# Four landing tiles, a summed turn of w_out, batch 0's Q scaled on ScalarE, and the quarters of the second stage in a row

## The chip, the cores and the metric

One core of a Trainium2 chip runs the whole program, one launch, all data in fp32. The metric is the device time of one execution in microseconds; three runs of the kernel before gave 676.89, 678.52 and 679.67 us (median 678.52). The profiled execution took 679.15 us.

Engines are named as in the profile: PE is TensorE (PEld its weight loads), DVE is VectorE, ACT is ScalarE, POOL is GpSimd, SP is SyncE, which here issues nearly all DMAs.

## What is computed

Three stages follow each other. Attention: 4 batches, 8 heads, 576 positions of 64 elements, with a causal mask over blocks of 64. Its output, as 2304 tokens of 512, goes through a dense layer with a maximum over three products, and that output through a mixture of experts with top-1 routing and a skip.

```python
scores = q @ k.T / sqrt(64), masked where block_i < block_j
x = softmax(scores) @ v                                # 2304 x 512
h = maximum(maximum(x @ w1, x @ w2), x @ w3)           # 2304 x 768
x2 = h @ w_out                                         # 2304 x 512
do = x2 @ w_skip > 0;  e = argmax(x2 @ w_gate);  gate = max softmax(x2 @ w_gate)
out = x2 + do * gate * (relu(x2 @ m2_w1[e]) @ m2_w2[e])  # 8 experts, 1024 wide
```

## The kernel before, in words

Tokens are handled in 9 chunks of 256. The scores of one head and up to 128 queries are a *half-unit*; the loop at L588 runs over the 192 half-units. For each one, `s_scores` multiplies Q by K (L295 for batch 0, L299 and L301 for the others), takes the negated maximum of each row (L306), applies the exponential with that maximum as bias (L314); `s_norm` scales the rows, `s_trans` turns them (L347), `s_pv` multiplies by V (L364). The half-units are two heads deep, and the four stages of neighbouring half-units overlap.

Precision: the dense layer splits each fp32 operand into a high and a low fp32r part. Batch 0's Q and K are used as plain fp32 (L295): K is loaded by L228 and Q by L229, the 64 rows and the 9 mask rows apart, so four DMAs for each of 12 (chunk, head pair) groups, eight of them with 256 queries and four with 64. For batch 0 the factor 0.125 is not on Q: it stands in the exponential's `scale` and on the maxima (L311 where a score has one part, folded into the minimum of L309 where it has two). For the other batches `prep` puts it on Q (L269).

The weights of the dense layer come as the raw 64-bit words of the host's arrays, 512 KB a piece: 18 pieces for w1 to w3 and 6 for w_out. `wprep` loads a piece into one of three landing tiles `raw` (L157, L164) and decodes it: ACT takes the absolute value (L146), DVE does four passes (L147 to L150), ACT copies the high part (L167), DVE subtracts the low one (L168). A landing tile is free again after L150. `routes` turns w_out (each 128 x 128 block by two matmuls, high and low part against a fp32r identity, L183), splits it and multiplies it by the router's weights, for the logits of later chunks.

Which work stands where: the attention phase is written in program order, with priorities, and a scheduler with its own model of durations places the instructions of each engine; each engine then runs its list in that order, and waits at the head of its list. The dense layer's steps (`moe_steps`, matmuls of L379 and L417) are handed out between half-units by a credit. SP's list of DMAs is also in order: a DMA waits there for its buffer to be free.

The second stage (`Moe2`) is in a fixed order. Seven tiles of 128 tokens each take four *quarters* of expert weights of 1 MB: s = 0 and 1 are the halves of the first layer, s = 2 and 3 those of the second; `self.seq` (L756) lists the 28 quarters, and loads, splits (ACT L838, DVE L843) and matmuls (L864, 12 a quarter) follow it. Between them `turn_h` turns the relu of a half (L852, copies L855 and L856) and `turn_x` turns a gathered tile of tokens. In the first tiles the order is (0,0) (0,1) (0,2) (1,0) (0,3) (1,1) and on; the relu of each half (L944, L946) stands on ACT behind the split of a quarter that comes five later.

## Time and profile before

| what | value |
|---|---|
| median of three runs | 678.52 us |
| profiled execution, its own time | 679.15 us |
| its span, first to last instruction | 677.4 us |
| busy in the span: PE, DVE, ACT, POOL | 654.1, 474.3, 384.7, 162.7 us |
| mean granted TensorE clock | 0.990 |

The profiled execution's time is 1.75 us longer than its span, and 0.63 us over the median. A busy PE is not PE at its peak: a matmul's record is longer than its step to the next one, so short waits are hidden in the busy time.

### The profile page before, as it was taken

What the parts mean: (1) busy time and instruction counts of PE and PEld (TensorE: products, weight loads), DVE (VectorE), ACT (ScalarE), POOL (GpSimd) and SP (SyncE); (2) the same over time, 40 slices, a digit from 0 to 9 for tenths busy, and PEclk for the clock granted to TensorE, in tenths of its full rate; (3) what the DMA queues carried; (4) which work ended last, traced back from release to release, by engine and by line L of the source; (5) the groups of instructions that cost most, each with busy time, mean ns of one, the idle gap of its engine ahead of it and who ended that gap; (6) DMA issues with size and microseconds to landing.
All of it is one profiled execution on the core that took longest, in us unless ns stands there. A gap on an engine that the chain in (4) does not pass through costs nothing. (4 is left out here: it accounts for less than half of the span.)

```text
span 677.4 us, 13700 instructions
## 1 busy us (share of the span) xinstructions
PE 654.1 (97%) x4820; PEld 553.7 (82%) x4820; DVE 474.3 (70%) x1405; ACT 384.7 (57%) x1012; POOL 162.7 (24%) x293
## 2 busy tenths in 40 slices
PE   6789999899999999999999999999999999999996
PEld 4548875689888998998997898889799889788885
DVE  4788998865677865776666656766675277599991
ACT  5677887757355554645444456454444163387861
POOL 2112122344113113221120224222021067221101
PEclk9979999999999999999999999999999999999999
DMA  7754444531222124223111132320210299399920
GB/s 201 183 167 137 149 149 145 180 78 56 79 74 57 52 68 149 78 60 110 28 28 60 60 91 82 122 82 21 83 37 6 78 337 328 107 323 379 380 96 12
DMA packets 78353, 83.18 MB, mean 123 GB/s; under 512 B 9150, under 2 KB 57694, under 8 KB 78282
## 3 DMA queue, kind: packets, MB, share of 16 engines
q1 hardware_dynamic: 76538, 79.19, 36.6%
q0 software_dynamic: 1744, 3.09, 1.3%
q8 instruction: 39, 0.64, 0.4%
q14 instruction: 32, 0.26, 0.1%
HBM read 71.58 MB, written 11.44 MB: 123 GB/s over the span
## 5 line engine op out<-in xcount | busy, mean ns | idle before, releaser
L379 PE MATMUL ps_h<-x,w 128*128 128x256 f32 x1944 | 277.1, 291 | 1.0 <-DVE hm L386 0.6
L379 PEld LDWEIGHTS ps_h<-x,w 128*128 128x128 f32 x1944 | 249.6, 192 | 11.1 <-issue 4.0
L314 ACT ACTIVATE p<-sc,nm 64x288 f32<-64x288 f32 (+9 forms) x192 | 95.4, 499 | 35.5 <-DVE nm L306 7.8
L306 DVE TENSOR_REDUCE nm<-sc 64x1 f32<-64x288 f32 (+9 forms) x192 | 85.2, 450 | 32.1 <-PE sc L301 20.4
L347 PE MATMUL tp<-cst_sb,p 128*128 128x128 f32 (+1 forms) x480 | 89.1, 280 | 5.7 <-ACT pT L349 3.4
L347 PEld LDWEIGHTS tp<-cst_sb,p 128*128 128x128 f32 (+1 forms) x480 | 57.0, 143 | 28.1 <-issue 12.5
L364 PE MATMUL pv<-pT,vt 128*64 128x128 f32 (+1 forms) x960 | 73.7, 277 | 0.7 <-ACT pT L349 0.7
L349 ACT COPY pT<-tp 128x256 f32<-128x256 f32 (+4 forms) x112 | 44.8, 400 | 42.9 <-PE tp L347 38.2
L843 DVE TENSOR_TENSOR lo<-raw,hi 128x1024 fp32r<-128x1024 f32 (+1 forms) x50 | 67.8, 1401 | 0.0
L391 POOL TENSOR_TENSOR h_l<-hm,h_h 128x256 fp32r<-128x256 f32 x52 | 45.8, 880 | 86.5 <-ACT h_h L390 86.1
L364 PEld LDWEIGHTS pv<-pT,vt 128*64 128x64 f32 x960 | 50.8, 139 | 17.4 <-issue 5.2
L274 POOL TENSOR_TENSOR kl<-kq,kh 64x512 fp32r<-64x512 f32 (+3 forms) x36 | 36.8, 1022 | 93.2 <-ACT kh L273 93.1
L838 ACT CAST hi<-raw 128x2048 fp32r<-128x2048 f32 x28 | 53.5, 1911 | 5.4 <-DMA raw<-in_m_w_dram 5.4
L351 DVE COPY pT<-tp 128x256 f32<-128x256 f32 (+4 forms) x80 | 35.4, 445 | 26.9 <-PE tp L347 24.3
L335 DVE TENSOR_SCALAR p<-p,r 128x320 f32<-128x320 f32 (+9 forms) x104 | 48.6, 468 | 4.5
L295 PE MATMUL sc<-kn,kq 73*64 73x288 f32 (+4 forms) x96 | 41.4, 532 | 8.3 <-DMA kq<-in_kq_dram 5.5
L299 PE MATMUL sc<-kh,q 128*128 128x288 f32 (+9 forms) x144 | 48.4, 341 | 0.0
L367 DVE TENSOR_TENSOR x<-pv,x 128x128 fp32r<-128x128 f32 (+1 forms) x80 | 21.7, 271 | 36.2 <-ACT x L366 35.7
L318 POOL MEMSET p<- 128x64 f32 (+1 forms) x96 | 14.4, 154 | 128.9 <-PE tp L347 107.2
L301 PE MATMUL sc<-kl,q 128*128 128x288 f32 (+9 forms) x144 | 44.1, 309 | 0.0
L417 PE MATMUL ps_y<-wo_h,h_h 128*128 128x512 f32 x108 | 43.9, 407 | 0.1
L417 PE MATMUL ps_y<-wo_h,h_l 128*128 128x512 f32 x108 | 42.8, 396 | 0.0
(206 smaller groups left out, 1045.2 us busy)
## 6 DMA issues: line engine op xcount, KB each, us to landing
raw<-in_m_w_dram SPq DMA_DIRECT2D x28, 1024.0 KB
raw<-in_w_dram SPq DMA_DIRECT2D x18, 512.0 KB
kq<-in_kqT_dram SPq DMA_DIRECT2D x16, 512.0 KB
vt<-in_v_dram SPq DMA_DIRECT2D x16, 320.0 KB
x<-y SPq DMA_DIRECT2D x18, 256.0 KB
out_dram<-y SPq DMA_DIRECT2D x18, 256.0 KB
raw<-in_w_out_dram SPq DMA_DIRECT2D x6, 512.0 KB
kq<-in_kqT_dram SPq DMA_DIRECT2D x8, 384.0 KB
```

Source lines behind the costliest of these rows:

```text
L299: nc.tensor.matmul(ps[:nq, 0:hi - lo], gd["q1"][:, j, q0:q0 + nq], gd["kh"][:, j, lo:hi], start=True, stop=False)
L306: nc.vector.tensor_reduce(nm[:nq, n:n + 1], pss[n][:nq, 0:hi - lo], axis=AX.X, op=ALU.max, negate=True)
L314: nc.scalar.activation(pt[:nq, lo:hi], pss[n][:nq, 0:hi - lo], AF.Exp, bias=nm[:nq, 0:1], scale=scale, accum_out=su[:nq, n:n + 1])
L335: nc.vector.tensor_scalar(pt, pt, r[:nq, 0:1], None, op0=ALU.mult)
L347: nc.tensor.transpose(tp[:, t, 0:nq], h["p"][:nq, (t0 + t) * P:(t0 + t + 1) * P], ident[:nq, :nq])
L349: nc.scalar.copy(pT[:, t0:t0 + n, 0:nq], tp[:, 0:n, 0:nq])
L364: nc.tensor.matmul(pv[64 * jj:64 * jj + 64, 0:nq], vt[:, t, 64 * jj:64 * jj + 64], hd[k - 1 + jj]["pT"][:, t, 0:nq], start=(t == 0), stop= ...
L379: nc.tensor.matmul(ps, a[:, d, :], x[:, d, :], start=(n == 0), stop=(n == 3 * ND - 1))
L391: (nc.vector if c == NCH - 1 and f >= NF - 2 else nc.gpsimd).tensor_tensor(h_l[:, f, :], prev, h_h[:, f, :], op=ALU.subtract)
L417: nc.tensor.matmul(ps, a[:, f, hs], x[:, f, :], start=(n == 0), stop=(n == 3 * NF - 1))
L838: self.nc.scalar.copy(self.w(q)[0], self.raw_of(q))
L843: eng.tensor_tensor(lo[:, :, a:b], raw[:, :, a:b], hi[:, :, a:b], op=ALU.subtract)
```

## The change

Five edits. (1) The decode has four landing tiles in place of three. (2) `routes` first adds the two parts of w_out on DVE (a tile `w`, 128 x 512 fp32) and turns the sum with one fp32 transpose a block; the fp32r identity and its copy on POOL are gone. (3) For batch 0, `prep` multiplies Q by 0.125 in place on ACT, once a group, with a high priority; `prep(0)` is called before the first loop step. The factor is gone from the exponential and the maxima: L311's instruction is gone, and L309 becomes a plain minimum. (4) The table of constants is loaded in three DMAs, the identity early, the triangle and the small tables later. (5) The quarters of the first tile stand in a row, (0,0) (0,1) (0,2) (0,3) (1,0) (1,1) (1,2) (2,0) (1,3) and on; the turns of the first tile's second half and of the second tile's tokens move with them.

```diff
--- before.py
+++ after.py
@@ -73,12 +73,11 @@
     table = dram.tile([NE * CAP, 2], F32, name="table")
     tdram = dram.tile([28, 2], I32, name="tdram")
 
-    cst_sb = const.tile([P, 2 * P + 8 + 10 + 8], F32, name="cst_sb")
+    cst_sb = const.tile([P, P + 8 + 10 + 8], F32, name="cst_sb")
     ident = cst_sb[:, 0:P]
-    rev8 = cst_sb[:, 2 * P:2 * P + 8]
-    fold = cst_sb[0:20, 2 * P + 8:2 * P + 18]
-    base8 = cst_sb[:, 2 * P + 18:2 * P + 26]
-    ident_r = const.tile([P, P], F32R, name="ident_r")
+    rev8 = cst_sb[:, P:P + 8]
+    fold = cst_sb[0:20, P + 8:P + 18]
+    base8 = cst_sb[:, P + 18:P + 26]
     tri = const.tile([P, P], BF16, name="tri")
     ones = const.tile([P, P], BF16, name="ones")
     tid = const.tile([P, NT // P], F32, name="tid")
@@ -95,7 +94,7 @@
 def _moe1_phase(tc, nc, const, small, g):
     kqT, kq0, v = g["kqT"], g["kq0"], g["v"]
     ident, rev8, fold, base8 = g["ident"], g["rev8"], g["fold"], g["base8"]
-    ident_r, wr_hl = g["ident_r"], g["wr_hl"]
+    wr_hl = g["wr_hl"]
     tri, ones, tid, cum16, wp = (g[n] for n in ("tri", "ones", "tid", "cum16", "wp"))
     wr_sb, x2, table, out, ids, steps = (g[n] for n in ("wr_sb", "x2", "table", "out", "ids", "steps"))
     ws = [g["w1"], g["w2"], g["w3"]]
@@ -132,6 +131,7 @@
         kh_all = [None] * NHP
         kl_all, q2_ring = [None] * NHP, [None] * 2
         raw_t = [apool.tile([P, 4 * P, 2], I32, tag=f"kl{i}", name=f"raw{i}") for i in range(3)]
+        raw_t.append(apool.tile([P, 4 * P, 2], I32, name="raw3"))
         dec_t = apool.tile([P, 2, 4 * P], I32, tag="kl3", name="dec_t")
         dec_t = [dec_t[:, 0], dec_t[:, 1]]
         dec_t += [apool.tile([P, 4 * P], I32, tag=f"q2{i}", name=f"dec{i}") for i in range(2)]
@@ -151,7 +151,7 @@
             return uf
 
         def wprep(k):
-            raw, dec = raw_t[k % 3], dec_t[k % 6]
+            raw, dec = raw_t[k % 4], dec_t[k % 6]
             if k < 18:
                 f, i = divmod(k, 3)
                 nc.sync.dma_start(
@@ -177,11 +177,11 @@
 
             turned = None
             for f in fs:
+                w = tmp.tile([P, DM], F32, tag="y", name="w")
+                nc.vector.tensor_tensor(w, wo[0][:, f], wo[1][:, f], op=ALU.add)
                 ps = ps_m.tile([P, ND, P], F32, tag="mo", name="pswt")
                 for d in range(ND):
-                    for n in range(2):
-                        nc.tensor.matmul(ps[:, d, :], wo[n][:, f, d * P:(d + 1) * P], ident_r,
-                                         start=(n == 0), stop=(n == 1))
+                    nc.tensor.transpose(ps[:, d, :], w[:, d * P:(d + 1) * P], ident)
                 wt = [tmp.tile([P, ND, P], F32R, tag="y", name=f"wt{n}") for n in range(2)]
                 nc.scalar.copy(wt[0], ps)
                 nc.vector.tensor_tensor(wt[1], ps, wt[0], op=ALU.subtract)
@@ -248,6 +248,9 @@
             gd = gdat[i]
             nq = qhi - qlo
             if b == 0:
+                q = gd["raw"][0:KN, 0:2, 0:nq]
+                with tc.high_priority(1000):
+                    nc.scalar.activation(q, q, AF.Copy, scale=0.125)
                 return
             if kh_all[hp] is None:
                 kh_all[hp] = apool.tile([P, 2, S], F32R, tag=f"kh{hp}", name=f"kh{hp}")
@@ -304,14 +307,11 @@
             nm = sm.tile([P, 2], F32, tag="nm", name="nm")
             for n, (lo, hi) in enumerate(parts):
                 nc.vector.tensor_reduce(nm[:nq, n:n + 1], pss[n][:nq, 0:hi - lo], axis=AX.X, op=ALU.max, negate=True)
-            scale = 0.125 if b == 0 else 1.0
             if len(parts) == 2:
-                nc.vector.tensor_scalar(nm[:nq, 0:1], nm[:nq, 0:1], nm[:nq, 1:2], scale, op0=ALU.min, op1=ALU.mult)
-            elif b == 0:
-                nc.vector.tensor_scalar(nm[:nq, 0:1], nm[:nq, 0:1], scale, None, op0=ALU.mult)
+                nc.vector.tensor_tensor(nm[:nq, 0:1], nm[:nq, 0:1], nm[:nq, 1:2], op=ALU.min)
             su = sm.tile([P, 2], F32, tag="su", name="su")
             for n, (lo, hi) in enumerate(parts):
-                nc.scalar.activation(pt[:nq, lo:hi], pss[n][:nq, 0:hi - lo], AF.Exp, bias=nm[:nq, 0:1], scale=scale,
+                nc.scalar.activation(pt[:nq, lo:hi], pss[n][:nq, 0:hi - lo], AF.Exp, bias=nm[:nq, 0:1],
                                      accum_out=su[:nq, n:n + 1])
             h["su"], h["parts"] = su, len(parts)
             if nk % P:
@@ -541,7 +541,8 @@
 
 
         load(0)
-        nc.sync.dma_start(out=g["cst_sb"], in_=g["cst"])
+        prep(0)
+        nc.sync.dma_start(out=ident, in_=g["cst"][:, 0:P])
         load_v(0)
         load(1)
 
@@ -550,15 +551,17 @@
             dv = dummy.rearrange("p (n t) -> p n t", t=2)
             nc.gpsimd.memset(dv[:, :, 0], BIG)
             nc.gpsimd.memset(dv[:, :, 1], 0.0)
+            trif = tmp.tile([P, P], F32, tag="y", name="trif")
+            nc.sync.dma_start(out=trif, in_=g["cst"][:, P:2 * P])
+            nc.sync.dma_start(out=g["cst_sb"][:, P:], in_=g["cst"][:, 2 * P:])
             nc.gpsimd.memset(ones, 1.0)
             nc.gpsimd.iota(tid, pattern=[[P, NT // P]], base=0, channel_multiplier=1,
                            allow_small_or_imprecise_dtypes=True)
-            nc.gpsimd.tensor_copy(ident_r, ident)
             nc.vector.tensor_copy(cum16, base8)
             nc.vector.tensor_scalar(ids, rev8, -1.0, 8.0, op0=ALU.mult, op1=ALU.add)
             nc.gpsimd.iota(steps, pattern=[[1, 28]], base=0, channel_multiplier=0,
                            allow_small_or_imprecise_dtypes=True)
-            nc.vector.tensor_copy(tri, g["cst_sb"][:, P:2 * P])
+            nc.vector.tensor_copy(tri, trif)
             nc.gpsimd.dma_start(out=table.rearrange("(p n) t -> p (n t)", p=P), in_=dummy)
             nc.sync.dma_start(out=wr_sb, in_=g["w_route"].rearrange("(c p) n -> p c n", p=P))
             nc.gpsimd.tensor_copy(wr_hl[:, :, 0:NG], wr_sb)
@@ -753,9 +756,9 @@
         self.loaded = 0
 
 
-        self.seq = [(0, 0), (0, 1), (0, 2)]
+        self.seq = [(0, s) for s in range(4)]
         for k in range(1, self.NS):
-            self.seq += [(k, 0), (k - 1, 3), (k, 1), (k, 2)]
+            self.seq += [(k, 0)] + [(k - 1, 3)] * (k > 1) + [(k, 1), (k, 2)]
         self.seq.append((self.NS - 1, 3))
         self.tt = plan.tile("tt", [P, self.NS, 2])
         self.ti = plan.tile("ti", [P, self.NS], I32)
@@ -920,7 +923,7 @@
             self.evict(ps, xT(k))
 
         for j, (k, s) in enumerate(self.seq):
-            if s == 0 and k > 0:
+            if s == 0 and k > 1:
                 turn_h(k - 1, 1)
             if s == 1 and k > 0:
                 turn_h(k, 0)
@@ -931,9 +934,9 @@
             mm(0, 6)
             if (k, s) == (0, 1):
                 turn_h(0, 0)
-            if (k, s) == (0, 2):
+            if (k, s) == (0, 3):
                 turn_x(1)
-            if (k, s) == (NS - 1, 2):
+            if s == 2 and k in (0, NS - 1):
                 turn_h(k, 1)
             mm(6, 12)
             if 6 <= j + 5 < len(self.seq):

```

The scheduler places the whole attention phase anew. Three places are shown, each first of the kernel before and then of the changed one.

SyncE's list of DMAs in the first microseconds, from the second head pair's last load on (`raw` are the landing tiles, `kn` and `kq` batch 0's K and Q, 64 or 9 rows):

```order
L229 DMA kq<-in_kq_dram 9x2x256
L240 DMA vt<-in_v_dram 128x2x128
L157 DMA raw_128<-in_w_dram 128x4x256
L157 DMA raw_129<-in_w_dram 128x4x256
L563 DMA wr_sb<-in_w_route_dram 128x4x10
L566 DMA aux_sb<-in_aux_dram 64x576
L157 DMA raw_130<-in_w_dram 128x4x256
L228 DMA kn_127<-in_kq_dram 64x2x256
L229 DMA kq<-in_kq_dram 64x2x256
```

```order
L229 DMA kq<-in_kq_dram 9x2x256
L240 DMA vt<-in_v_dram 128x2x128
L157 DMA raw_127<-in_w_dram 128x4x256
L157 DMA raw_128<-in_w_dram 128x4x256
L555 DMA trif<-in_cst_dram 128x128
L556 DMA cst_sb<-in_cst_dram 128x26
L566 DMA wr_sb<-in_w_route_dram 128x4x10
L569 DMA aux_sb<-in_aux_dram 64x576
L157 DMA raw_129<-in_w_dram 128x4x256
L157 DMA raw_130<-in_w_dram 128x4x256
L228 DMA kn_126<-in_kq_dram 64x2x256
L229 DMA kq<-in_kq_dram 64x2x256
```

A fourth piece and two loads of constants now stand ahead of the last head pair's K and Q.

ScalarE's list at its start (`kq` is Q, `sc` the scores, `p` their exponentials):

```order
L314 ACT_TABLE_LOAD
L314 ACTIVATE p,su<-sc,nm 128x128 x2
L333 ACTIVATE p<-p,r 128x128
L314 ACTIVATE p,su<-sc,nm 128x256
L333 ACTIVATE p<-p,r 128x128
```

```order
L253 ACT_TABLE_LOAD
L253 ACTIVATE kq<-kq 73x512
L314 ACTIVATE p,su<-sc,nm 128x128 x2
L333 ACTIVATE p<-p,r 128x128
L253 ACTIVATE kq<-kq 73x512
L314 ACTIVATE p,su<-sc,nm 128x256
```

The scale of Q stands ahead of the first exponential, and the load of the function table belongs to it; in the program both come behind a wait for the DMAs of the first Q, where the table load before waited for nothing.

TensorE's list at the second stage's second and following quarters (`psy` collects the second layer, `h` is a relu to be turned, `xgs` the gathered tokens):

```order
L864 MATMUL psy<-hi_8021,Two_h 128x512 x4
L864 MATMUL psy<-hi_8021,Two_l 128x512 x2
L852 MATMUL ps_x<-cst_sb,xgs_8504 128x128 x4
L864 MATMUL psy<-hi_8021,Two_l 128x512 x2
L864 MATMUL psy<-lo_8293,Two_h 128x512 x4
L852 MATMUL pst_8034<-cst_sb,h_8692 128x128 x4
L864 MATMUL psa_8031<-hi_8022,Two_h 128x512 x4
```

```order
L867 MATMUL psy<-hi_7991,Two_h 128x512 x4
L867 MATMUL psy<-hi_7991,Two_l 128x512 x2
L855 MATMUL pst_8004<-cst_sb,h_8662 128x128 x4
L867 MATMUL psy<-hi_7991,Two_l 128x512 x2
L867 MATMUL psy<-lo_8263,Two_h 128x512 x4
L867 MATMUL psy<-hi_7992,Two_h 128x512 x4
L867 MATMUL psy<-hi_7992,Two_l 128x512 x2
L855 MATMUL ps_x<-cst_sb,xgs_8474 128x128 x4
```

The turn of the gathered tokens stands a quarter later, and the turn of the relu half a quarter earlier, than before. Counted over TensorE's lists up to the first score of batch 1 (L299 before, L302 now), 228 of the 1944 matmuls of L379 stand ahead of it before and 312 now; ahead of the last such score it is 1662 and 1682.

## Rows read from the trace of the kernel before

**Rows 1.** The head of the page: the span, and the engines' busy time in us with its share of the span and the number of instructions.

```profile
span 677.4 us, 13700 instructions
...
PE 654.1 (97%) x4820; PEld 553.7 (82%) x4820; DVE 474.3 (70%) x1405; ACT 384.7 (57%) x1012; POOL 162.7 (24%) x293
```

**Rows 2.** Busy time by stretch of the span (batch 0 and the decode; the rest of attention; the dense layer's rest; the end of the dense layer and the first quarters; the rest of the second stage): us, busy us and instructions of each engine, granted clock, DMA share, GB/s.

```profile
0.00:124.70 124.70, 111.06 (x670) 77.66 (x670) 101.36 (x289) 93.90 (x256) 26.81 (x68) 0.96 0.53 158
124.70:521.60 396.90, 394.53 (x3284) 350.89 (x3284) 265.58 (x939) 208.05 (x661) 95.75 (x193) 1.00 0.25 73
521.60:543.00 21.40, 21.40 (x161) 18.18 (x160) 6.03 (x23) 6.23 (x17) 1.46 (x2) 1.00 0.24 84
543.00:595.00 52.00, 50.09 (x343) 44.52 (x342) 35.17 (x85) 23.04 (x31) 26.70 (x19) 1.00 0.73 255
595.00:677.40 82.40, 77.00 (x367) 62.44 (x365) 66.14 (x71) 53.44 (x51) 12.01 (x11) 0.98 0.65 237
```

**Rows 3.** The same view for four stretches of 5 us within the first.

```profile
15.00:20.00 5.00, 4.84 (x19) 2.74 (x16) 4.60 (x15) 3.56 (x12) 0.94 (x4) 1.00 1.11 237
20.00:25.00 5.00, 1.96 (x7) 1.00 (x5) 2.43 (x10) 1.88 (x8) 0.76 (x1) 1.00 0.48 137
40.00:45.00 5.00, 3.59 (x10) 1.24 (x8) 4.26 (x14) 3.54 (x9) 0.42 (x2) 0.80 0.42 137
45.00:50.00 5.00, 5.00 (x17) 3.03 (x16) 3.57 (x11) 4.29 (x11) 0.67 (x2) 0.50 0.49 158
```

**Rows 4.** The timeline around the stall at 21 us: start, duration, engine, line, operation, tiles, and in brackets the idle time before and what ended it (SPq is a DMA's issue).

```profile
17.31 0.39 SPq L157 DMA_DIRECT2D raw<-in_w_dram  x1
...
21.21 0.76 PE L295 MATMUL sc<-kn,kq 73*128 73x128 f32 x2 [0.18 <-DMA kq<-in_kq_dram]
...
24.22 0.66 ACT L146 ACTIVATE dec<-raw 128x512 f32<-128x512 f32 x1 [3.12 <-DMA raw<-in_w_dram]
...
25.19 0.47 PE L347 MATMUL tp<-cst_sb,p 128*128 128x128 f32 x1 [3.00 <-ACT pT L349]
```

**Rows 5.** Groups of instructions in the first 124.7 us: count, busy us, mean ns of one, idle time of the engine just before them and what ended it.

```profile
L146 ACT ACTIVATE dec<-raw 128x512 f32<-128x512 f32 x16 | 10.9, 681 | 8.2 <-DMA raw<-in_w_dram 7.7 <-DMA raw<-in_w_out_dram 0.5
...
L146 ACT ACTIVATE dec_t<-raw 128x512 f32<-128x512 f32 x8 | 5.3, 667 | 3.9 <-DMA raw<-in_w_dram 2.6 <-DMA raw<-in_w_out_dram 1.3
```

**Rows 6.** The timeline of the start.

```profile
0.74 1.28 ACT L314 ACT_TABLE_LOAD   x1 [0.74 <-PEq L1028]
...
5.29 3.21 PE L295 MATMUL sc<-kn,kq 73*128 73x128 f32 x8 [5.29 <-DMA kq<-in_kq_dram]
...
6.76 0.37 ACT L314 ACTIVATE p<-sc,nm 128x128 f32<-128x128 f32 x1 [4.74 <-DVE nm L311]
```

**Rows 7.** Groups over the whole span, shapes kept apart, columns as in the group above: ScalarE's and VectorE's passes that are nearest to those added and removed.

```profile
L269 ACT ACTIVATE q<-kq 128x512 fp32r<-128x512 f32 x16 | 10.1, 633 | 1.6 <-PE sc L299 1.0
L168 DVE TENSOR_TENSOR w<-dec,w 128x512 fp32r<-128x512 f32 x12 | 8.2, 685 | 0.1
L147 DVE TENSOR_SCALAR dec<-dec 128x512 f32<-128x512 f32 x16 | 6.7, 419 | 5.5 <-ACT dec L146 5.4
...
L311 DVE TENSOR_SCALAR nm<-nm 128x1 f32<-128x1 f32 x32 | 4.7, 147 | 0.2
```

**Rows 8.** One line's instructions each: count, duration in ns (least, median, most), first and last start in us, shapes.

```profile
L269 ACT ACTIVATE q<-kq x36: 297/525/649, 119.7 to 490.8; 128x512 fp32r<-128x512 f32 x16, 128x384 fp32r<-128x384 f32 x8, 128x256 fp32r<-128x256 f32 x8, 128x128 fp32r<-128x128 f32 x4
...
L299 PE MATMUL sc<-kh,q x144: 192/350/487, 124.7 to 521.4; 128*128 128x288 f32 x32, 128*64 128x64 f32 x16, 128*128 128x192 f32 x16, 128*128 128x320 f32 x16
```

**Rows 9.** Groups between 124.6 and 521.6 us: the dense layer's matmuls.

```profile
L379 PE MATMUL ps_h<-x,w 128*128 128x256 f32 x1434 | 201.9, 288 | 0.6 <-DVE hm L386 0.6
```

**Rows 10.** TensorE's timeline where w_out's first block row is turned (eight matmuls, of which the first and the last), and where a tile `y` is turned by four fp32 transposes; the row behind each is where TensorE goes on.

```profile
143.98 0.22 PE L183 MATMUL pswt<-ident_r,wo_h 128*128 128x128 f32 x1
...
144.71 0.28 PE L183 MATMUL pswt<-ident_r,wo_l 128*128 128x128 f32 x1
144.83 0.81 PE L379 MATMUL ps_h<-x,w 128*128 128x256 f32 x5
...
125.05 0.66 PE L485 MATMUL psyt<-cst_sb,y 128*128 128x128 f32 x4
125.46 0.72 PE L379 MATMUL ps_h<-x,w 128*128 128x256 f32 x4
```

**Rows 11.** The timeline of the second stage's first quarters, TensorE and ScalarE.

```profile
583.62 1.09 PE L864 MATMUL psa<-hi,x0h 128*128 128x512 f32 x4
...
584.54 1.09 PE L864 MATMUL psa<-hi,x0l 128*128 128x512 f32 x4
...
588.90 1.91 ACT L838 CAST hi<-raw 128x2048 fp32r<-128x2048 f32 x1
...
590.56 0.63 PE L864 MATMUL psy<-hi,Two_l 128*128 128x512 f32 x2
590.71 0.59 ACT L946 ACTIVATE h<-psa 128x512 f32<-128x512 f32 x1
...
592.23 0.63 PE L852 MATMUL ps_x<-cst_sb,xgs 128*128 128x128 f32 x4 [1.05 <-DMA xgs<-x,tg]
```

**Rows 12.** TensorE's waits from 124.7 us to the end, longest in total first: who waited for what, us in total, times, the longest.

```profile
PE ps_x L852 <- DMA xgs<-x,tg: 1.0, 1, 1.0
PE tp L347 <- DVE x L367: 1.0, 1, 1.0
```

## Prediction

> **What bounds the kernel now.** I read the page's head first [rows 1], then the busy time by stretch [rows 2]. TensorE is busy for 654.1 of 677.4 us, so a change can win in two ways only: less work for TensorE, or less of its empty time. The reader is to see in the stretches where that empty time lies. From 124.7 to 521.6 us TensorE is idle for 2.4 us of 396.9. In the first 124.7 us, where batch 0's scores and the decode of the weights run, it is idle for 13.6 us (124.70 - 111.06), and only 228 of the 1944 matmuls of L379 get done there. Three engines share that stretch without any being full: VectorE 101.4, ScalarE 93.9, TensorE 111.1 of 124.7 us. That pattern means chains of short dependent steps in lists that run in order: whoever stands at the head of a list and waits holds up everything behind it.
>
> The timeline shows such a case [rows 4]. SyncE issues the fourth piece of weights at 17.31 us, when the first of three landing tiles is free; ScalarE's first pass over it stands at the head of its list from 21.1 to 24.22 us and waits for those bytes; the copy that TensorE needs is behind it, and TensorE stands still for 3.0 us until 25.19. Over the whole decode ScalarE's first passes waited 8.2 + 3.9 = 12.1 us for landings [rows 5]. The DMA engines are full only for a while: share 1.11 from 15 to 20 us, 0.48 from 20 to 25 [rows 3]. So the landing tiles, rather than the bandwidth, limit the decode after the first 20 us.
>
> **The change part by part.** The sum is made against the profiled execution's 679.15 us: the span of 677.4 plus 1.75 around it, which no edit touches. It is 0.63 us above the median of the runs, 678.52.
>
> *Start, +1.9.* TensorE's first score waits for the DMA until 5.29 us, while ScalarE's table load, 1.28 us, was long done [rows 6]. Now the table load comes behind the wait for the same DMA, and Q's scale behind that. The scale's nearest row is the same operation on the other batches' Q: 633 ns for 512 elements [rows 7]. 1.28 + 0.63 = 1.9. Ends: 0, if the following DMA wait swallows it, and 1.9.
> The Trainium skill ("ScalarE: Activation LUTs", section "What ACT_TABLE_LOAD costs") puts a drain of about 1.38 us beside the load of about 1.28 us. The row agrees on the load with 1.28; what stood behind it in the kernel before was a wait of 4.74 us, so no drain can be seen. With the drain the start would cost 3.3 in place of 1.9.
>
> *Landings, -4.0.* With a fourth tile, a piece is asked for one piece earlier. A wait at the head of ScalarE's list goes when its piece has landed by then; what is late next is VectorE's four passes, which free the tile. The ends are 0 and the 12.1 us above. I take a third, since the first waits lie where the DMA engines are full and a wait of ScalarE need not be one of TensorE: of TensorE's 13.6 us of idle time 5.29 lie before its first matmul and 3.0 at this stall.
>
> *Scale off the maxima, -2.3.* 32 passes of 147 ns [rows 7] leave VectorE, 4.7 us; the minimum of two parts costs one pass before and after. VectorE is busy for 81% of the stretch; I take half, ends 0 and -4.7.
>
> *Scale on Q, +3.1.* Eight groups of 512 elements at 0.633 and four of 128 at 0.297 [rows 7, 8]: 5.1 + 1.2 = 6.3 us more for ScalarE, busy for 75% of the stretch. Half, ends 0 and +6.3. The other passes keep their place and length.
> The Trainium skill ("ScalarE: Activation LUTs", section "Rules for kernel authors") says that multiplications belong on VectorE. The rows agree on the length: VectorE's pass over 512 elements of fp32 takes 419 ns where ScalarE's takes 633 [rows 7]. By the rule alone, the move would lose 12 passes' difference; here it also replaces 32 passes by 12, so that it decides neither way.
>
> *Dense-layer work moved forward, +3.0 and -7.9.* By the lists, 84 more matmuls of L379 stand ahead of batch 1's first score, at 124.7 us in the trace [rows 8], and only 20 more ahead of its last one at 521.4. One such matmul takes 201.9 / 1434 = 0.141 us of TensorE in the full stretch [rows 9], so 84 are 11.8 us. They are paid for before 124.7 us, in part out of empty time (13.6 us idle there), and are missing behind it, where TensorE has no idle time left to lose. Ends for the payment: 0 and 11.8; I take a quarter, 3.0. Ends for what comes back: 0, if that stretch is set by the chain of scores, and 11.8; I take two thirds, 7.9, since TensorE is busy for 99% of it but a busy record hides short waits.
>
> *Turn of w_out, -2.6.* Eight matmuls take from 143.98 to 144.83, 0.85 us; four fp32 transposes of a tile of the same size from 125.05 to 125.46, 0.41 us [rows 10]. Six block rows: 6 x 0.44 = 2.6. VectorE gets 6 adds of 0.685 [rows 7], 4.1 us, beside TensorE's dense work, where VectorE is busy for 67% (265.6 of 396.9); I cost them at 0. Without that cover they would take 4.1, so ends -2.6 and +1.5. POOL's copy of the identity and the split of the table of constants touch nothing that TensorE waits for.
>
> *Quarters in a row, +0.3.* Now TensorE loses time at the turn of the gathered tokens: at 0.23 us a matmul (four from 583.62 to 584.54) it is ready at 590.56 + 2 x 0.23 = 591.02 and starts at 592.23 [rows 11]: 1.2 us, the longest wait after 124.7 us [rows 12]. Half a turn and six matmuls later the tokens have landed, so that goes. Two new waits come. The relu of the half that now stands there ends at 590.71 + 0.59 = 591.30, 0.3 us late. And behind quarter (1,0) stands at once the turn of its own relu, with no quarter between: TensorE has to wait for a pass of 0.59 and a hand-over at least (together some 0.85 us, the hand-over an estimate from the 0.3 above), and longer if the casts of 1.91 us that stand ahead of the relu on ScalarE are late. I take 1.2. 0.3 + 1.2 - 1.2 = +0.3; ends -1.2 and +2.
>
> Sum: 1.9 - 4.0 - 2.3 + 3.1 + 3.0 - 7.9 - 2.6 + 0.3 = -8.5. That makes 679.15 - 8.5 = 670.65 for a run like the profiled one and 670.0 against the median; I give 670.5 between them.
>
> **Not in the sum.** The granted clock falls to 0.50, the 1.2 GHz level, at about 43 us and is there through 45 to 50 us, after a stretch in which TensorE had done little [rows 3]. If that goes, the matmuls of some 10 us run at twice the rate, at most 5 us gained; if it comes twice, at most 5 lost. I take 0.
>
> **Rivals.**
> *The forward work is worth nothing.* From 124.7 to 521.6 us the chain of scores, maximum, exponential and turn could set the time, with the dense matmuls as filler; less filler then means more empty time. For it: a busy record hides waits. Against it: 2.4 us of idle in 396.9. The -7.9 goes: 679.15 - 0.6 = 678.5.
> *ScalarE becomes the bound of the first stretch (slower).* It would carry 93.9 + 6.3 + 1.8 (each 36 of the moved matmuls bring two passes: 84 / 36 x 2 at 0.4, between the least and the median pass of L269 [rows 8]) = 102 us between 5.3 and 124.7, 85%; waits at its head come on top. If it is late throughout, no landing is won, the scales count in full and the moved work is paid in full: 1.9 + 6.3 + 11.8 - 7.9 - 2.6 + 0.3 = +9.8, 689; with half of that mechanism, 680 to 684. It decides once ScalarE is over some 95% busy up to batch 1's first score. For it: VectorE, the fuller one, is relieved, ScalarE is loaded. Against it: 25% of its stretch is free.
> *The fourth tile brings nothing.* It asks for 0.5 MB when the DMA engines are already full [rows 3], ahead of the last head pair's Q: at 237 GB/s that is 2.2 us later for Q, and now a pass of ScalarE waits for it. Landings cost +2.2 in place of -4.0: 676.8.
> *Everything comes back.* All 11.8 us behind batch 0 and 8 of the 12.1 us of landings: 670.65 - 3.9 - 4.0 = 662.7.
>
> **How the numbers follow.** Forecast 0.55, own range 665 to 675.5; forward work worth nothing 0.17; ScalarE the bound 0.11; fourth tile without effect 0.08; everything 0.09. The range of 663 to 680.5 leaves out ScalarE's worse half, a little of the best case and the tails of a list placed anew. About 0.5% is what a measurement here can tell from no change; that is 3.4 us, so the line to faster is at 675.1 and to slower at 681.9. Faster: nearly all of the forecast, the best case, and some of the third and first rivals, 0.67. Slower: ScalarE the bound and a bad case of the first rival, 0.14. The rest, 0.19.
>
> **What the profile after would show.** The first score at 7.2 us. ScalarE's waits for landings well under 12.1 us in total. Batch 1's first score at about 126 to 128 us, with 312 matmuls of L379 before it, and its last one 5 us or more earlier than 521.4. The turn of w_out at 0.41 us a block row. No wait for gathered tokens, and one of about 1 us at the turn behind (1,0). The prediction is wrong if batch 1's first score is later than 136 us (ScalarE), or comes at 128 while the last one stays at 521 (work only moved).

## The result, and the profile after

The changed kernel takes 688.87 us in the median of 4 runs (685.6 to 690.3), beside 678.3 for the kernel before (676.89 to 679.67): the ratio is 1.0147, with a 95% interval of 1.011 to 1.0183. It is slower by about 10 us, where 8 us less were forecast. The profiled execution of after took 685.6 us and is the fastest of its four; its span is 683.8 us, 6.4 more than [rows 1]. One execution each of the runs e4, e9 and e11 below took 2.1 to 3.4 ms, and no ratio holds it.

The head of after's page, and then the busy time by stretch (columns as in [rows 2]; the second bound is moved to batch 1's first score, the third to just behind its last, the others by 6.4 us):

```profile
span 683.8 us, 13686 instructions
...
PE 659.4 (96%) x4796; PEld 555.2 (81%) x4796; DVE 475.7 (70%) x1379; ACT 390.3 (57%) x1024; POOL 160.0 (23%) x292
```

```profile
0.00:139.30 139.30, 127.19 (x783) 92.87 (x784) 108.72 (x293) 104.90 (x283) 31.03 (x71) 0.96 0.51 155
139.30:524.40 385.10, 383.09 (x3168) 337.73 (x3167) 258.26 (x909) 202.89 (x648) 90.63 (x189) 1.00 0.24 70
524.40:549.40 25.00, 24.60 (x174) 20.11 (x173) 7.71 (x35) 7.80 (x18) 3.03 (x4) 1.00 0.23 86
549.40:601.40 52.00, 48.10 (x314) 42.72 (x313) 35.30 (x73) 21.50 (x28) 23.36 (x18) 0.97 0.69 242
601.40:683.80 82.40, 76.45 (x365) 61.78 (x363) 65.71 (x70) 53.26 (x50) 11.93 (x11) 1.00 0.66 241
```

TensorE has 24 matmuls less and is busy 5 us longer. A busy record holds waits inside it, so the account is made by milestones. The rows for it are single lines' instructions in after: batch 1's scores (they answer to L299 of [rows 8]) and the dense layer's matmuls, count, duration in ns (least, median, most), first and last start.

```profile
L302 PE MATMUL sc<-kh,q x144: 192/340/505, 139.3 to 524.2; 128*128 128x288 f32 x32, 128*64 128x64 f32 x16, 128*128 128x192 f32 x16, 128*128 128x320 f32 x16
...
L379 PE MATMUL ps_h<-x,w x1944: 274/283/775, 20.9 to 578.5; 128*128 128x256 f32 x195
```

| stretch | before, us | after, us | difference |
|---|---|---|---|
| to the first score | 5.3 | 7.2 | +1.9 |
| from there to batch 1's first score | 119.4 | 132.1 | +12.7 |
| batch 1's first score to its last | 396.7 | 384.9 | -11.8 |
| last score to the last dense matmul (572.0; 578.5) | 50.6 | 54.3 | +3.7 |
| from there to the end of the span | 105.4 | 105.3 | -0.1 |
| sum | 677.4 | 683.8 | +6.4 |

In this profiled run what was won and lost in attention cancels nearly to nothing; what is left over is the start and the end of the dense layer. Other executions of the same list lose more in attention (see "One list, several executions"). 312 matmuls of L379 stand ahead of batch 1's first score (228 before), 1682 ahead of its last (1662). More than these came forward: ahead of the first score TensorE has 113 instructions more (783 against 670), 84 of them of L379, and the other 29 belong to the turn of `y`, the logits, the routing and the first turn of w_out.

**The start** went as forecast. Columns as in [rows 6]:

```profile
5.18 1.28 ACT L253 ACT_TABLE_LOAD   x1 [5.18 <-DMA kq<-in_kq_dram]
6.48 0.63 ACT L253 ACTIVATE kq<-kq 73x512 f32<-73x512 f32 x1
...
7.16 2.93 PE L298 MATMUL sc<-kn,kq 73*128 73x128 f32 x8 [7.16 <-ACT kq L253]
```

The Trainium skill ("ScalarE: Activation LUTs", section "What ACT_TABLE_LOAD costs") puts a drain of about 1.38 us beside the load. Here the load has 1.28 us and the next pass starts 0.02 us behind it, so no drain shows, and the start is 1.9 us later, not 3.3.

**The decode** is through 13.4 us earlier: its last first pass starts at 98.5 us instead of 111.9. The groups that answer to [rows 5]:

```profile
L146 ACT ACTIVATE dec<-raw 128x512 f32<-128x512 f32 x16 | 10.9, 680 | 7.5 <-DMA raw<-in_w_dram 5.7 <-DMA raw<-in_w_out_dram 1.8
L146 ACT ACTIVATE dec_t<-raw 128x512 f32<-128x512 f32 x8 | 5.5, 682 | 1.8 <-DMA raw<-in_w_dram 1.1 <-DMA raw<-in_w_out_dram 0.6
```

The waits for landings fell from 12.1 to 9.3 us, and the stall of [rows 4] is gone. Yet batch 1 starts 14.6 us later.

**The end of the dense layer.** TensorE's waits behind 139.3 us (they answer to [rows 12]: who waited for what, us in total, times, the longest), then the timeline at the longest of them, then the windows view of the 4 us behind it:

```profile
PE ps_h L379 <- DVE hm L386: 2.5, 1, 2.5
PE pv L364 <- ACT pT L349: 1.3, 1, 1.3
PE ps_h L379 <- ACT ha L383: 1.1, 1, 1.1
PE pst L855 <- ACT h L947: 0.7, 1, 0.7
```

```profile
566.37 7.41 DVE L846 TENSOR_TENSOR lo<-raw,hi 128x1280 fp32r<-128x1280 f32 x2
...
571.79 0.37 ACT L383 COPY ha<-ps_h 128x256 f32<-128x256 f32 x1 [2.82 <-PE ps_h L379]
573.70 0.41 DVE L386 TENSOR_TENSOR hm<-ps_h,ha 128x256 f32<-128x256 f32 x1
574.17 4.63 PE L379 MATMUL ps_h<-x,w 128*128 128x256 f32 x24 [2.48 <-DVE hm L386]
```

```profile
574.00:578.00 4.00, 3.83 (x19) 3.83 (x20) 1.39 (x4) 0.41 (x1) 0.00 (x0) 0.57 1.02 391
```

The copy that the maximum needs is done at 572.16 us, but VectorE stands in two splits of expert weights, one behind the other, until 573.78. The maximum is late, TensorE waits 2.5 us, and then works for 3.4 us at a granted clock of 0.50, the 1.2 GHz level. In before two maxima stand between one split and the next, and TensorE runs 144 matmuls without a wait:

```profile
554.76 17.55 PE L379 MATMUL ps_h<-x,w 128*128 128x256 f32 x144 [0.33 <-ACT ha L383]
...
561.15 2.81 DVE L843 TENSOR_TENSOR lo<-raw,hi 128x1280 fp32r<-128x1280 f32 x1
...
563.88 0.41 DVE L386 TENSOR_TENSOR hm<-ps_h,ha 128x256 f32<-128x256 f32 x1
...
564.73 3.34 DVE L843 TENSOR_TENSOR lo<-raw,hi 128x1280 fp32r<-128x1280 f32 x1
```

The gathered-token wait of [rows 12] is gone; 0.7 us behind quarter (1,0) stand in its place, as forecast.

### The profile page after: what moved, and what is told of

It is laid out like the page before. It is cut to its first block, busy times and chain, and to the rows that moved or that the text cites. A ratio compares the mean times of both kernels' runs of the same rounds, so it can differ in the third digit from the quotient of the medians.

```text
span 683.8 us, 13686 instructions
## 1 busy us (share of the span) xinstructions
PE 659.4 (96%) x4796; PEld 555.2 (81%) x4796; DVE 475.7 (70%) x1379; ACT 390.3 (57%) x1024; POOL 160.0 (23%) x292
## 5 line engine op out<-in xcount | busy, mean ns | idle before, releaser
L379 PE MATMUL ps_h<-x,w 128*128 128x256 f32 x1944 | 281.9, 293 | 5.4 <-DVE hm L386 2.5
L379 PEld LDWEIGHTS ps_h<-x,w 128*128 128x128 f32 x1944 | 251.8, 193 | 18.0 <-issue 4.6
L309 DVE TENSOR_REDUCE nm<-sc 64x1 f32<-64x288 f32 (+9 forms) x192 | 85.0, 450 | 50.5 <-PE sc L304 34.5
L347 PE MATMUL tp<-cst_sb,p 128*128 128x128 f32 (+1 forms) x480 | 92.6, 282 | 3.2 <-ACT pT L349 3.2
L364 PE MATMUL pv<-pT,vt 128*64 128x128 f32 (+1 forms) x960 | 77.0, 278 | 1.3 <-ACT pT L349 1.3
L347 PEld LDWEIGHTS tp<-cst_sb,p 128*128 128x128 f32 (+1 forms) x480 | 57.9, 144 | 24.4 <-issue 10.5
L846 DVE TENSOR_TENSOR lo<-raw,hi 128x1024 fp32r<-128x1024 f32 (+1 forms) x50 | 69.2, 1428 | 0.0
L391 POOL TENSOR_TENSOR h_l<-hm,h_h 128x256 fp32r<-128x256 f32 x52 | 43.2, 831 | 89.7 <-ACT h_h L390 86.4
L302 PE MATMUL sc<-kh,q 128*128 128x288 f32 (+9 forms) x144 | 47.6, 337 | 0.2
L318 POOL MEMSET p<- 128x64 f32 (+1 forms) x96 | 14.6, 156 | 125.1 <-PE tp L347 121.8
L417 PE MATMUL ps_y<-wo_l,h_h 128*128 128x512 f32 x108 | 42.5, 398 | 0.0
```

Of the source, the lines that this page charges most:

```text
L302: nc.tensor.matmul(ps[:nq, 0:hi - lo], gd["q1"][:, j, q0:q0 + nq], gd["kh"][:, j, lo:hi], start=True, stop=False)
L309: nc.vector.tensor_reduce(nm[:nq, n:n + 1], pss[n][:nq, 0:hi - lo], axis=AX.X, op=ALU.max, negate=True)
L347: nc.tensor.transpose(tp[:, t, 0:nq], h["p"][:nq, (t0 + t) * P:(t0 + t + 1) * P], ident[:nq, :nq])
L364: nc.tensor.matmul(pv[64 * jj:64 * jj + 64, 0:nq], vt[:, t, 64 * jj:64 * jj + 64], hd[k - 1 + jj]["pT"][:, t, 0:nq], start=(t == 0), stop= ...
L379: nc.tensor.matmul(ps, a[:, d, :], x[:, d, :], start=(n == 0), stop=(n == 3 * ND - 1))
L417: nc.tensor.matmul(ps, a[:, f, hs], x[:, f, :], start=(n == 0), stop=(n == 3 * NF - 1))
```

## The experiments

All ratios are to the kernel before, measured beside it on the same chip, with 95% intervals. "L379 ahead" counts the dense matmuls ahead of batch 1's first and last score.

### e1_no_q_scale, e2_three_tiles, e3_only_q_scale, e4_no_row: one edit out, or one alone

```diff
 e1 = after, without edit 3 (the scale on the maxima again)
-                    nc.scalar.activation(q, q, AF.Copy, scale=0.125)
 e2 = after, with three landing tiles
-        raw_t.append(apool.tile([P, 4 * P, 2], I32, name="raw3"))
 e3 = before, with edit 3 alone
+                    nc.scalar.activation(q, q, AF.Copy, scale=0.125)
 e4 = after, with the quarters in the order of before
```

> The changed kernel without edit (3): maxima and exponentials carry the factor again, Q is not scaled; four landing tiles, the summed turn and the quarters in a row stay. Theory S (the scale of Q on ScalarE, and what it does to the lists, is what loses): first score at 5.3 us again, batch 1's first score 8 us or more earlier than the changed kernel's 139.3, time 670 to 676. Theory P (the dense work pulled forward by the four tiles is paid in full before batch 1 and that is the loss): batch 1's first score stays at 135 or later, time 680 to 686. Theory T (the loss is the end of the dense layer at 574 us, where TensorE waited 2.5 us and its clock fell): no such wait here, since the list of VectorE stands there as before; time 4 to 5 us under the changed kernel, whatever the first stretch does.

> The changed kernel with three landing tiles in place of four, all else as changed. Theory P: less work is pulled forward (296 matmuls ahead of batch 1's first score by the list, in place of 312, 228 before), so batch 1's first score comes 2 us earlier and the time hardly moves, 684 to 690. Theory S: still slower than before, 684 to 690, and ScalarE's waits for landings go back to some 12 us. If the fourth tile is what loses: 676 to 680.

> The kernel before with edit (3) alone. Theory S: 684 to 690, first score at 7.2 us, batch 1's first score 6 us or more late for the work ahead of it (288 matmuls against 228: 60 x 0.14 = 8.4 us are not lost but moved). Theory P or T: 676 to 681.

> The changed kernel with the quarters in their old order. Its attention phase is the same list as the changed kernel's, so the first 540 us and the wait near 574 us should repeat. If the quarters in a row cost what was forecast (+0.3) the time is that of the changed kernel within 1 us: 686 to 690. If they lose 2 us or more at the relu behind (1,0), 684 to 686. A wait for gathered tokens of some 1 us should be back near 597 us.

| kernel | ratio | first score, L379 ahead | last score, L379 ahead | last dense matmul |
|---|---|---|---|---|
| e1 | 0.9994 (0.993 to 1.0058) | 136.5, 300 | 523.4, 1662 | 574.1 |
| e2 | 0.9999 (0.9938 to 1.006) | 136.8, 296 | 525.9, 1686 | 575.5 |
| e3 | 0.9993 (0.9935 to 1.005) | 132.0, 288 | 522.5, 1686 | 572.2 |
| e4 | 1.0117 (1.0051 to 1.0183) | 140.5, 312 | 529.0, 1682 | 582.1 |

No single edit is the loss: take out the Q scale or the fourth tile, and the kernel is level with before, as far as intervals of 0.6% (4 us) either way can tell. Of these lists only the one that has both is slower (after and e4, whose TensorE order up to the last score is the same). e1, e2 and e3 all have far more dense work ahead of batch 1 than before and show no loss in the end. None has the late pair of splits; in e1 no two stand together, in e2 and e3 two do some ten us earlier, 5.0 us in all, and TensorE waits 0.6 and 1.0 us behind them.

Of the expectations, those for e3 (676 to 681 us; 680.97) and e4 (689.9 us, and a wait of 1.4 us for gathered tokens is back) came true. In e1 theory P's first score (136.5 us) and time (680.4 us) did, but before took 680.95 us beside it, so the work paid ahead of batch 1 is not a loss there. e2's 682.0 us lies between the ranges given.

### e5_tail_written and e6_before_tail_written: the last chunk in written order

```diff
-        for n in range(3 * NF):
-            m2.before_step(n)
-            run_moe()
-        m2.before_step(3 * NF)
         with tc.manual_schedule():
+            for n in range(3 * NF):
+                m2.before_step(n)
+                run_moe()
+            m2.before_step(3 * NF)
             run_moe()
```

> The kernel after, with the dense layer's last chunk put in the order in which it is written (VectorE's split then never stands in a pair ahead of two maxima); attention's list is the same, 312 matmuls of L379 before batch 1's first score, 1682 before its last. Theory T (the tail's list cost about 4 us: two splits of 7.4 us, a wait of 2.5 us and the clock's fall behind it): the stretch from the start of the expert weights to the last dense matmul runs at 0.130 us a matmul in place of 0.149, no wait of TensorE over 1 us there, and the time is about 4 us under the kernel after, 684 to 686. Rival R (the pair of splits was empty time anyway, the loss lies in attention): the rate falls, but the time stays within 1.5 us of the kernel after's 688.9. Batch 1's first score at 139 to 141 us by both.

> The kernel before with the same written order in the last chunk; its own list had no pair of splits ahead of two maxima. Theory T: no change, within 1 us of before (the rate was 0.130 already). Rival R2 (written order is better or worse by itself, whatever the pair): a change of over 2 us either way, and then e5 shows the same change and not the pair's.

Theory T was wrong in both, and rival R2 (the written order is worse by itself) holds: 1.0314 (1.0269 to 1.0359) and 1.0194 (1.0159 to 1.0229), 11 and 13 us worse than the kernels they were made from. Batch 1's first score in e5, 144.2 us, lies outside of the 139 to 141 as well. The written order has no pair of splits, but something worse at the head of VectorE's list. VectorE's waits in e6 from 545 to 584 us, then TensorE's:

```profile
DVE ti L803 <- DMA tt<-table: 6.8, 1, 6.8
```

```profile
PE ps_h L379 <- DVE hm L386: 10.0, 4, 6.3
```

An index pass waits 6.8 us for a table from memory, the maximum behind it is late, and TensorE loses 10.0 us. As a test of the pair it failed; it shows that VectorE's order decides the time of this stretch, and that a wait at its head can cost TensorE nearly its whole length (6.3 of 6.8 us).

### e9_last_split_pool and e10_before_last_split_pool: the second split of the pair to GpSimd

```diff
-            self.split_lo(q, (self.nc.vector, 0, 320), (self.nc.gpsimd, 320, 512))
+            self.split_lo(q, (self.nc.gpsimd if q == 5 else self.nc.vector, 0, 320), (self.nc.gpsimd, 320, 512))
```

> The kernel after, with VectorE's share of the one split that stands second in its pair (quarter 5) given to GpSimd; attention's list is the same. Theory T (VectorE's pair of splits, 7.4 us at its list's head, makes TensorE wait 2.5 us for a maximum and the clock falls behind it): that wait and the fall go, the stretch from the start of the expert weights to the last dense matmul runs at 0.130 to 0.135 us a matmul in place of 0.149, and the time is 3 to 4 us under the kernel after, 684.5 to 686. Rival R (the loss there is made up by a later start of the second stage in any case, or GpSimd's longer pass becomes the next wait): time within 1 us of the kernel after's 688.8.

> The kernel before with the same edit; its list has no pair of splits there. Theory T: within 1 us of before, the rate stays at 0.130. If it gains 3 us or more here too, the gain of e9 is the lighter VectorE's and not the pair's; if it loses, GpSimd's longer pass is late for TensorE.

e9: 1.0112 (1.007 to 1.0154); e10: 1.0015 (0.998 to 1.005), no change. TensorE's waits in e9 from 545 us on:

```profile
PE ps_l L401 <- ACT h_h L390: 1.0, 1, 1.0
PE pst L855 <- ACT h L947: 0.7, 1, 0.7
PE ps_h L379 <- ACT ha L383: 0.6, 1, 0.6
```

The 2.5 us wait and the clock's fall behind it are gone. From the last score to the last dense matmul e9 takes 49.6 us (527.3 to 576.9) where after takes 54.3: 4.7 us less. 1.4 of them go again at once (from there to the last matmul of ps_y 12.8 us, in after 11.4), since TensorE waits 1.0 us for the last hidden block. What makes that block late is a pass of VectorE's:

```profile
573.99 4.24 DVE L391 TENSOR_TENSOR h_l<-hm,h_h 128x256 fp32r<-128x256 f32 x1 [0.47 <-ACT h_h L390]
```

In after the same pass takes 0.43 us; here GpSimd's two splits run beside it, 4.74 us from 573.21. So rival R is right in part: GpSimd's longer work becomes the next wait. From the last score to the last matmul of ps_y e9 takes 62.4 us, after 65.7 and e7 below, which has the pair too, 63.9. So the pair cost some 2 to 3 us of the total by the traces, and the same edit gains nothing where there is no pair. The times alone don't show it: e9's 686.61 us lies between T's 686 and R's 688.8, and its interval overlaps that of after. A ratio of 1.011 is left that the tail doesn't explain.

### e7_table_early: the start's delay taken away

```diff
+        warm = sm.tile([P, 1], F32, tag="r", name="warm")
+        with tc.high_priority(2000):
+            nc.vector.memset(warm, 0.0)
+            nc.scalar.activation(warm, warm, AF.Copy)
         load(0)
         prep(0)
```

> The kernel after, with one more activation of one column, at the head of ScalarE's list, that loads the table while the first transfer is on its way. First score at about 5.9 us in place of 7.2, since only Q's scale (0.6 us) stands behind the transfer then. Theory P (the first stretch is one in-order chain in which every delay at the start is passed on): batch 1's first score and the end come 1.3 us earlier, and the time is 1 to 1.5 us under the kernel after. Rival S (the delay is swallowed by the next waits for the DMA at 15 to 25 us): batch 1's first score within 0.4 us of the kernel after's, time unchanged.

1.0166 (1.0129 to 1.0202). The first score comes at 6.07 us, 1.1 earlier, and batch 1's first at 140.5, no earlier than in after. The 17th score still comes 1.0 us earlier (14.3 us, beside 15.3 to 15.4 in the four other executions of this list that are given below); the 33rd doesn't (32.9, beside 31.7 to 33.1). So rival S's account holds: the delay at the start is swallowed by then. Its bound of 0.4 us at batch 1's first score was too narrow, since the same list spreads over 4.9 us there.

### e8_half_chunk0 and e12_less_forward: dense matmuls taken out

```diff
 e8 = before, e12 = after with the other condition
+                nd = ND // 2 if c == 0 else ND
+                nd = ND // 4 if c == 1 and 3 * f + i < 7 else ND
-                for d in range(ND):
+                for d in range(nd):
...
```

> The kernel before, in which the dense layer's chunk 0 contracts over half of its input (108 fewer matmuls of L379 of 1944, all of them ahead of batch 1's first score, about 96 fewer there because 12 more of another chunk come forward): part of the sum is left out. It shows what a dense matmul costs in the first stretch. Theory F (there they are paid in full, since the empty time comes from waits that dense work doesn't fill): batch 1's first score about 96 x 0.141 = 13.5 us earlier than 124.7, at 110 to 112. The prediction's step (paid for a quarter): 3 to 4 us earlier, 120 to 122. The time falls by 108 x 0.141 = 15.2 us or more than the shift, if the rest is unchanged.

> The kernel after, in which the first seven groups of chunk 1 (the 84 matmuls that now stand ahead of batch 1's first score) contract over a quarter of their input, 63 matmuls of L379 fewer in all and, by the order, 261 ahead of that score in place of 312: part of the sum is left out, and with it tokens may be routed otherwise, so only attention's stretch is read. Theory Z (behind the decode TensorE is full and each dense matmul costs 0.141 us): batch 1's first score 51 x 0.141 = 7.2 us earlier than in the kernel after (139.3 to 144.2 in its list's four profiled runs), at 132 to 137. The prediction's step (a quarter is paid): 1.8 us earlier, 137.5 to 142.

In e8 both ranges fell (110 to 112 us and 120 to 122; 124.2). In e12 theory Z's fell (132 to 137; 140.7), and the step's 137.5 to 142 holds, which says little: that is nearly where after's list lies by itself, 139.3 to 144.2. Batch 1's scores in e8, and then in e12:

```profile
L299 PE MATMUL sc<-kh,q x144: 192/347/481, 124.2 to 520.2; 128*128 128x288 f32 x32, 128*64 128x64 f32 x16, 128*128 128x192 f32 x16, 128*128 128x320 f32 x16
```

```profile
L302 PE MATMUL sc<-kh,q x144: 192/353/507, 140.7 to 531.0; 128*128 128x288 f32 x32, 128*64 128x64 f32 x16, 128*128 128x192 f32 x16, 128*128 128x320 f32 x16
```

96 matmuls fewer (13.5 us at 0.141) bring batch 1 forward by 0.5 us, 51 fewer (7.2 us) by nothing. Part is lost to the clock. The windows view of e8 (the first row is the fall that before has at 43 us), and of e12:

```profile
35.00:46.00 11.00, 11.00 (x34) 6.57 (x32) 9.22 (x27) 7.81 (x23) 2.69 (x5) 0.53 0.36 109
96.00:104.00 8.00, 5.75 (x35) 4.02 (x35) 7.30 (x18) 6.31 (x13) 0.97 (x2) 0.57 0.57 187
```

```profile
133.00:147.00 14.00, 13.40 (x80) 11.27 (x81) 6.74 (x24) 7.40 (x23) 6.87 (x11) 0.51 0.35 90
```

With less dense work TensorE stands still more (18.1 us against 13.6 up to batch 1), and falls once more to 0.50: for 6.8 us from 96.9 us in e8, in a wait of 2.1 us, and for 13.7 us from 133.1 us in e12, 7.6 of them ahead of batch 1's first score. Even if each such microsecond cost a half, that is 3.4 and 3.8 us, not 13 and 7. What is left, 10 us in e8, is more than the spread of before's list (121.3 to 124.7); the 3.4 us left in e12 lie within that of after's (139.3 to 144.2). So in e8 the matmuls alone are not what the stretch costs; e8's are chunk 0's, though, which stand ahead of the moved ones. (The second stage got other tokens in these two, so their totals aren't compared.)

### e13_held_back and e14_held_back_no_q_scale: the moved work behind batch 1 again

```diff
 e13 = after, e14 = e1, each with
+                if c == 1 and 3 * f + i < 7:
+                    nc.tensor.matmul(ps, kl_all[0][:, 0, 0:P], xh[:, 0, :], start=True, stop=True)
                 for d in range(ND):
-                credit += NM / per_chunk[c] * (0.8 if c == 1 else 1)
+                credit += NM / per_chunk[c] * (0.8 if c == 1 else 1 if c > 2 else 0 if groups[i][1] == 0 else 1.5)
```

> The kernel after, in which each of chunk 1's first seven groups begins with one matmul that reads batch 1's k (its sum is overwritten by the next): the groups can't go ahead of batch 1. By the order 242 rows of L379 and its kind stand ahead of batch 1's first score in place of 312 (26 of them chunk 1's); the tail's list has no late pair of splits. Theory Z (the moved work is paid where it stands and comes back where it is missing): batch 1's first score 8 to 10 us earlier than the 139.3 to 144.2 of the kernel after's list, at 130 to 133, its last score where it was, 524 to 529, time 683 to 686 (the 4 us of the tail). Rival W (moving it ahead is itself the loss: it holds up batch 0's last scores): first score the same 130 to 133, but the last one 8 us earlier too, 515 to 520, time 674 to 678. Rival V (not TensorE's matmuls but the other engines' lists set this stretch): first score stays at 137 or later.

> The same held-back groups in the kernel after without edit 3 (e1): 232 ahead of batch 1's first score, e1 had 300 and 136.5 us. Theory Z: first score at 127 to 129, last at 523 to 526, time within 1.5 us of e1's ratio of 0.9994 to before. Rival W: time 5 us or more under before, 0.992 or less: then this is the version that beats both kernels. Rival V: first score later than 134.

e13: 1.0124 (1.0058 to 1.0189); e14: 1.0057 (1.0028 to 1.0085). Batch 1's scores in e13 and in e14:

```profile
L302 PE MATMUL sc<-kh,q x144: 192/347/481, 133.4 to 528.5; 128*128 128x288 f32 x32, 128*64 128x64 f32 x16, 128*128 128x192 f32 x16, 128*128 128x320 f32 x16
```

```profile
L299 PE MATMUL sc<-kh,q x144: 191/348/481, 128.6 to 524.7; 128*128 128x288 f32 x32, 128*64 128x64 f32 x16, 128*128 128x192 f32 x16, 128*128 128x320 f32 x16
```

Theory Z is right in both about the direction: batch 1 starts 6 to 8 us earlier than in the kernels they were made from (139.3 and 136.5), and its last score comes where it came there (524.2 to 531.2 in after's list; 523.4 in e1). e14's scores lie within Z's ranges; e13's first, 133.4, is 0.4 behind its range, and the gains are less than the price of the matmuls held back (70 and 68, 9.9 and 9.6 us at 0.141). W falls, and so do V's 137 and 134. It is not the clock that sets these two apart from e12: they too run at 0.50 ahead of batch 1, for 6.8 us from 120.6 us (e13) and 10.2 us from 117.1 us (e14). Here the groups' other passes on VectorE, ScalarE and GpSimd were held back with the matmuls, and batch 1 came earlier. That speaks for the whole group of work, and not TensorE's share, as what is paid and given back; it isn't shown alone, since the edit also changes the credit that hands out the next chunk's work. In time, e13 is 1 us above the 683 to 686 that Z gave, and e14 is 4 us above e1's ratio, its interval overlapping e1's: holding the work back is no gain. e13's list has no late pair of splits either, and still it is as slow as after within the intervals: its last score is as late.

### e11_turn_and_row: without the tile and the scale

```diff
 e11 = after, with three landing tiles and without edit 3
-        raw_t.append(apool.tile([P, 4 * P, 2], I32, name="raw3"))
-                    nc.scalar.activation(q, q, AF.Copy, scale=0.125)
```

> The kernel before with the summed turn of w_out, the constants in three loads and the quarters in a row, without the fourth landing tile and without the scale on Q. By the order 264 matmuls of L379 stand ahead of batch 1's first score (before 228, after 312). Theory Z (work moved forward behind the decode is paid in full and comes back in full; the turn gives 2.6 us; the fourth tile and the scales give nothing): batch 1's first score about 5 us later than before, the last score 2 to 3 us earlier, time 2.5 us under before, 0.996. Rival M (every list with more dense work ahead of batch 1 loses): time 1 to 3 us over before.

1.0038 (1.0001 to 1.0076): Z's gain of 2.5 us isn't there; rival M's 1 to 3 us over before is. Batch 1's first score comes at 132.9 us with 264 ahead (Z's 5 us later than before would be 130), its last at 527.3 with 1686 (Z had it earlier than before).

### One list, several executions

TensorE's order up to batch 1's last score is the same in after, e4, e5, e7 and e9, and in before, e6 and e10. So the profiles give several executions of each list:

| list | batch 1's first score, us | its last score, us |
|---|---|---|
| before | 124.7; 121.3; 122.3 | 521.4; 520.0; 519.4 |
| after | 139.3; 140.5; 144.2; 140.5; 139.7 | 524.2; 529.0; 531.2; 529.3; 527.3 |

The mean of the first is 122.8 and 140.8, of the last 520.3 and 528.2. The profiled run of after is the best of its five here. So attention costs after's list some 8 us rather than the 2.8 of the table above. The 20 more dense matmuls behind it (2.8 us) and the cheaper turn of w_out (2.6) nearly cancel there. In e4, e7 and e9 a wait of 1.0 to 1.3 us of the routing's turn for ScalarE's copy of the logits, at about 425 us, and 3.4 us at the granted clock of 0.50 behind it are part of that; before's list has neither.

## Why the prediction was wrong

*The step that failed is "Dense-layer work moved forward, +3.0 and -7.9", in its first half, the payment.* By stretches, the sum had +1.7 up to batch 1's first score (1.9 - 4.0 - 2.3 + 3.1 + 3.0), -10.5 from there to its last (-7.9 - 2.6), nothing to the last dense matmul and +0.3 behind it. Measured: +14.6, -11.8, +3.7 and -0.1; by the means of several executions the first two are +18.0 and -10.1. So what comes back was sized well. The payment was not: it was charged a quarter of 11.8 us, 3.0, because TensorE is idle for 13.6 us in the first stretch, and measured it is the whole, +12.7 us from the first score to batch 1's, for the 84 matmuls and the 29 other instructions that came with them. Two errors made it. The empty time lies early (5.3 us before the first matmul, 3.0 at 22 us, others around 34 to 42 us), while the moved groups stand behind the end of the decode: the windows view of before's last 14.5 us ahead of batch 1, where 1.35 us were empty, and then after's group of the 84, between 115.7 and 139.3 us:

```profile
110.20:124.70 14.50, 13.15 (x89) 7.39 (x89) 12.15 (x32) 12.20 (x37) 3.72 (x9) 1.00 0.35 99
```

```profile
L379 PE MATMUL ps_h<-x,w 128*128 128x256 f32 x84 | 13.0, 295 | 1.6 <-DVE r L330 1.3 <-DVE ex L445 0.3
```

And it priced a moved group by its matmuls alone: in e8 and e12 matmuls taken out gave back next to nothing, part of it lost to the clock, while in e13 and e14 groups moved whole gave back 6 to 8 us, most of their price.

*What was missing is the tail's order.* No term of the sum and no rival had the last chunk, since no edit touches it. But the scheduler placed VectorE's splits anew: e9 gives back 4.7 us of the stretch, and 2 to 3 of the total.

*Start, +1.9*: right, 1.87 at the first score; by e7 nothing of it is left at the 33rd score, so its place in the time was the lower end, 0.

*Landings, -4.0*: the waits fell by 2.8 us and the decode ended 13.4 us earlier, but no time came of it. With three tiles (e2, 0.9999) the kernel is faster than with four (1.0147). Nor is the tile alone what pulls dense work forward: the turn and the row by themselves have 264 matmuls ahead of batch 1 (e11), Q's scale by itself 288 (e3), and the fourth tile brings e2's 296 to 312. The third rival, the tile without effect, is right that it wins nothing, but its mechanism, a later Q for the last head pair, wasn't tested.

*Scale, -2.3 and +3.1*: alone on before it costs nothing that can be told (0.9993, e3). Beside the fourth tile it costs some 5 us with the work held back (e14 to e13, 1.0057 to 1.0124, intervals that overlap) and some 10 us without (e1 to after, 0.9994 to 1.0147), of which the pair of splits, which e1 hasn't, has 2 to 3. No fixed price per pass, as the sum took it, describes that; the runs don't settle through which waits it comes.

*Turn of w_out, -2.6*: as far as the trace goes right, six groups of four transposes that take TensorE 0.35 to 0.59 us each from the first's start to the next instruction's, 2.8 us together, where the 48 matmuls took 6.2. In the total it can't be seen: e11, which has it, is 0.4% slower than before.

*Quarters in a row, +0.3*: right, 105.3 us against 105.4 behind the last dense matmul; e4 lies within after's interval.

*The clock, 0*: right at the place it was said of, 10.2 us at 0.50 from 43.0 us on before and from 41.8 us on after; the 3.4 us at 574 us belong to the tail.

*The first rival*, forward work worth nothing, asked that nothing come back behind batch 1's first score, and falls by the -11.8.

*The slower rival*, ScalarE as the bound, gave 680 to 689 and the time fell into it, but not by its mechanism: ScalarE is busy for 104.9 of 139.3 us, 75%, where it asked for 95%. That the number lay in its range is luck. The test "batch 1's first score later than 136 us" was met for another reason, so it didn't single out a mechanism.

What stays open: of the 10 us, the tail has 2 to 3, and some 8 lie in attention's list, 520.3 us at its last score before and 528.2 after, by the means. Fully paid and given back, the moved work alone would leave nearly nothing there. Which of the list's waits it is, beyond the one at 425 us, no run settled. No kernel tried was faster than before; e1, e2, e3 and e10 are level with it.

## What to carry to other kernels

When a scheduler places work anew, look up where the moved instructions now stand, not only how many of them stand ahead of a point: empty time pays only for work that lies in it. Work moved across a milestone in a kernel whose engines are nearly full is paid there and given back behind it, and the net of that is about nothing. And read the whole new order, the stretches that no edit touches too: here two passes that came to stand together on VectorE, more than 400 us behind the edits, cost 2 to 3 of the 10 us lost.
